# First batch of a Fourier filter and SwiGLU kernel: copies to VectorE, tables behind x in SyncE's queue, stores to ScalarE's queue

## The chip, the cores and the metric

One core of a Trainium2 chip. The time is the device time of one execution in microseconds (us), as the median of the runs of a kernel; the span of a profiled execution is about 1.8 us shorter than its time. "Faster" means by more than 2%.

## The reference, cut to what matters

```python
# x: 8 batches x 3008 x 256, filter: 1505 x 256 (real and imaginary)
X = np.fft.rfft(x, axis=1)
y = np.fft.irfft(X * (filt_r + 1j * filt_i)[None], n=3008, axis=1)
t = y.reshape(8 * 3008, 256)
g = t @ w_gate                                  # 256 -> 1536
out = (g / (1 + np.exp(-g)) * (t @ w_val)) @ w_out
```

The kernel does the Fourier transform as matmuls in three steps (3008 = 47 x 64), with a round trip through two DRAM tensors, d1 and d2, to turn the data between the steps. The dense part (gate, value, output projection) is done with a Strassen scheme of seven products. For batches 1 to 7 the spectral part is hidden in gaps of the dense part of the batch before. For batch 0 it stands alone at the front, and that front is all that this case is about.

## The kernel before

The first step, for each of 16 units: one fp32 matmul (`pa`, which the trace records as two overlapping passes, 1.06 us each in batch 0), a copy out of PSUM, a store to d1.

```python
def stage1(self, u):
    ...
    p1 = spool0 if self.b == 0 and u % 2 else t1pool
    t1 = p1.tile([NK, NV, C], FP32, ..., tag="t1", bufs=2)      # four tiles in all for batch 0
    ps = fps.tile([128, NV, C], FP32, ..., tag="f")             # two PSUM banks
    nc.tensor.matmul(out=ps[0:NK], lhsT=wf_t, rhs=self.x.pop(u), start=True, stop=True)
    nc.scalar.copy(out=t1, in_=ps[0:NK])
    queue = nc.scalar if self.b == 1 else nc.gpsimd
    queue.dma_start(out=self.d1_rows[:, ts(u, NV), :], in_=t1)
```

The tables and the filter of batch 0: three parts of one table transfer (1 MB) and four filter transfers, all 15 issued by ScalarE.

```python
def load_tables(self, parts=3):
    ...
    for i in range(parts):
        nc.scalar.dma_start(out=tb[:, ts(i, n)], in_=de_dram[:, ts(i, n)])
        for rows, view in filter_parts():                       # real: rows 0-63, imaginary: 64-127
            nc.scalar.dma_start(out=f[rows, ts(i, n), :], in_=view(n * i, n))
```

The middle step reloads d1 (`t2`), multiplies (`pb`), filters on VectorE (four operations into `p` and `q`), adds on GpSimd, multiplies back (`pc`), copies on ScalarE (`g`) and stores to d2:

```python
def stage2a(self, u):
    ...                                                         # pb into ps
    for h in (lo, hi):
        nc.vector.tensor_tensor(out=pt[h], in0=ps[h], in1=fr, op=ALU.mult)
    nc.vector.scalar_tensor_tensor(out=qt[lo], in0=ps[hi], scalar=-1.0, in1=fi, ...)
    nc.vector.tensor_tensor(out=qt[hi], in0=ps[lo], in1=fi, op=ALU.mult)
    add(nc.gpsimd, pt, pt, qt)

def stage2b(self, u):
    ...                                                         # pc into ps
    nc.scalar.copy(out=g, in_=ps)
    for p in range(2):
        queue = nc.scalar if self.b == 0 and p else nc.gpsimd   # one store each
        queue.dma_start(out=self.d2[...], in_=g[64 * p:64 * p + 64])
```

The weights come as 64-bit floats in 18 pieces and are rounded to fp32 on the chip (five VectorE operations, two on ScalarE, five on GpSimd each); two pieces are rounded before the middle step, two after the last step (`pd`), the others in the dense part.

```python
for i in range(4):
    spec.load_x(i)                     # SyncE's queue
spec.load_tables()                     # ScalarE's queue
load_weights(0); load_weights(1)       # SyncE's queue
nc.sync.dma_start(out=wi_t, in_=wi_dram.ap())
for u in range(N_ONE):
    spec.stage1(u)
for _ in range(2):
    round_weights(todo.pop(0))         # each also loads the piece after next
...                                    # middle step, stage2b three units behind stage2a
for i in range(2):
    spec.load_t4(0, i)
for step in range(4):
    spec.stage3(0, step)
for _ in range(2):
    round_weights(todo.pop(0))
```

## Time and profile before

3151.23 us, median of 4 runs (3150.08 to 3152.27); three runs had 3150.79. The front, read from the timeline (T0 is the start of the middle step's first matmul):

| milestone before | us |
|---|---|
| first matmul of the first step | 11.11 |
| first, last copy out of its PSUM banks (ScalarE) | 41.95, 68.85 |
| T0 | 77.33 |
| last filter operation on VectorE | 117.47 |
| first matmul of the last step | 133.18 |
| start of the dense part | 140.08 |
| end of the span | 3150.0 |

So there are 140 us that a better front can shorten, and 3009.9 us of dense part behind them. The prediction below shows the lines that lead to this. Two windows of 5 us while x and the tables load (columns: window, length, busy us and count of PE, PEld, DVE, ACT, POOL, then granted clock, share of the DMA engines busy, GB/s):

```profile
20.00:25.00 5.00, 0.00 (x0) 0.00 (x0) 0.00 (x0) 0.00 (x0) 0.00 (x0) 1.00 1.04 238
35.00:40.00 5.00, 0.00 (x0) 0.00 (x0) 0.76 (x2) 0.00 (x0) 0.00 (x0) 1.00 1.14 274
```

The granted clock of 1.00 in such early windows should not be read as full speed: the two passes of one `pa` take 1.99 us at 11.11 us and 1.02 us at 2542.22 us of the same trace.

### The profile page before, as it was taken

The page shows a single profiled execution, that of the slowest core. Times are in us where ns is not written, and L with a number is a line of the kernel's source. Part 1 is how long each engine was busy: PE and PEld are TensorE (multiplying, and loading weights), DVE is VectorE, ACT ScalarE, POOL GpSimd, SP SyncE. Part 2 cuts the span into 40 slices and gives each one's busy share as a digit, 9 for nine tenths or more (in the row PEclk, how much of TensorE's full clock was granted, in tenths as well). Part 3 has the DMA queues.
Part 4 walks back from the last instruction along what each step waited for, and adds up shares of the span by engine and source line. Part 5 has one row for each costly group of instructions (what it writes and reads, how often), then busy time and mean ns, then how long its engine had stood idle before and what let it go on. Part 6 is the DMA issues. An engine that isn't in the chain of part 4 may idle for free.

```text
span 3150.0 us, 41042 instructions
## 1 busy us (share of the span) xinstructions
PE 3042.9 (97%) x15488; PEld 2236.8 (71%) x15488; DVE 1461.6 (46%) x2331; ACT 1149.9 (37%) x2086; POOL 1409.8 (45%) x1634
## 2 busy tenths in 40 slices
PE   3689999999999999999999999999999999999999
PEld 1456777677777777777777677777777677777776
DVE  0665544345533445335543455434554445544443
ACT  1244333433334333433334433333333433333333
POOL 1475554345543345434444445434544345533333
PEclk9799999999999999999999999999999999999999
DMA  8432322213222223122222222221321212210000
GB/s 191 113 119 88 87 64 61 70 54 90 68 57 63 71 64 87 50 70 64 77 60 60 67 81 67 62 65 54 87 74 52 71 55 77 64 31 21 21 5 17
DMA packets 122481, 212.50 MB, mean 67 GB/s; under 512 B 23670, under 2 KB 68214, under 8 KB 121426
## 3 DMA queue, kind: packets, MB, share of 16 engines
q1 hardware_dynamic: 91388, 128.58, 14.8%
q0 software_dynamic: 25024, 70.29, 7.7%
q10 hardware_dynamic: 5872, 11.01, 1.5%
q8 instruction: 122, 2.00, 0.3%
q14 instruction: 75, 0.61, 0.1%
HBM read 134.81 MB, written 74.97 MB: 67 GB/s over the span
## 4 chain that ended last, share of the span: by engine, by line
PE 80%; POOL 8%; DVE 5%; issue 3%; DMA 2%; ACT 2%; SPq 0%; POOLq 0%; ACTq 0%; DVEq 0%
PE wA_v L419 15%; PE wA_g L419 15%; PE wA_o L483 7%; PE wE_v L419 7%; PE wE_g L419 7%; PE wE_o L483 7%; PE wF_o L483 4%; PE wF_g L419 4%; PE pd L380 4%; PE wF_v L419 3%; PE pa L319 3%; POOL o L162 3%; POOL h L165 3%; PE pc L360 3%; PE pb L340 2%
## 5 line engine op out<-in xcount | busy, mean ns | idle before, releaser
L419 PE MATMUL wA_v<-y,wv_t 128*128 128x376 f32 x1536 | 613.8, 481 | 8.6 <-ACT u_v L428 6.5
L419 PE MATMUL wA_g<-y,wg_t 128*128 128x376 f32 x1536 | 615.7, 483 | 0.9 <-ACT u_g L428 0.9
L165 POOL TENSOR_TENSOR h<-h 128x376 f32<-128x376 f32 x576 | 567.1, 985 | 28.8
L162 POOL TENSOR_TENSOR h<-h 128x376 f32<-128x376 f32 x192 | 189.0, 984 | 705.9 <-PE wE_v L419 387.7
L428 ACT COPY u_g<-wA_g 128x376 f32<-128x376 f32 x576 | 269.5, 468 | 587.3 <-PE wA_g L419 585.0
L419 PEld LDWEIGHTS wA_v<-y,wv_t 128*128 128x128 f32 x1536 | 290.7, 191 | 205.8 <-DVE h L441 15.8
L483 PEld LDWEIGHTS wA_o<-wo_t,h 128*128 128x128 f32 x3456 | 407.5, 193 | 16.5 <-issue 0.6
L483 PE MATMUL wA_o<-wo_t,h 128*128 128x128 f32 x3456 | 418.7, 276 | 0.0
L419 PEld LDWEIGHTS wA_g<-y,wg_t 128*128 128x128 f32 x1536 | 282.1, 191 | 167.2 <-issue 28.0
L446 ACT ACTIVATE s<-s 128x1128 f32<-128x1128 f32 x192 | 219.5, 1143 | 375.9 <-DVE s L162 375.9
L448 DVE TENSOR_TENSOR h<-s,h 128x1128 f32<-128x1128 f32 x192 | 256.3, 1335 | 123.4 <-ACT s L446 123.2
L419 PE MATMUL wE_v<-y,wv_t 128*128 128x376 f32 x768 | 307.9, 483 | 3.4 <-DVE h L162 3.4
L419 PE MATMUL wE_g<-y,wg_t 128*128 128x376 f32 x768 | 306.3, 481 | 1.8 <-DVE s L162 1.2
L428 ACT COPY u_v<-wA_v 128x376 f32<-128x376 f32 x576 | 272.2, 473 | 69.9 <-PE wA_v L419 66.0
L162 DVE TENSOR_TENSOR s<-u_g,wE_g 128x376 f32<-128x376 f32 x384 | 209.0, 544 | 176.8 <-ACT u_g L428 174.9
L483 PE MATMUL wE_o<-wo_t,h 128*128 128x128 f32 x2304 | 282.1, 277 | 7.5 <-DVE o L162 7.5
L162 DVE TENSOR_TENSOR s<-u_g,wF_g 128x376 f32<-128x376 f32 x192 | 104.5, 544 | 393.7 <-PE wF_g L419 375.4
L483 PE MATMUL wF_o<-wo_t,h 128*128 128x128 f32 x2304 | 278.6, 275 | 0.0
L483 PEld LDWEIGHTS wE_o<-wo_t,h 128*128 128x128 f32 x2304 | 267.7, 192 | 14.1 <-DVE o L162 13.6
L483 PEld LDWEIGHTS wF_o<-wo_t,h 128*128 128x128 f32 x2304 | 267.8, 192 | 0.3
L162 DVE TENSOR_TENSOR h<-u_v,wE_v 128x376 f32<-128x376 f32 x384 | 209.1, 545 | 28.1 <-ACT u_v L428 5.1
L419 PEld LDWEIGHTS wE_v<-y,wv_t 128*128 128x128 f32 x768 | 146.3, 191 | 102.1 <-DVE h L162 5.1
(82 smaller groups left out, 3222.7 us busy)
## 6 DMA issues: line engine op xcount, KB each, us to landing
t<-d SPq DMA_DIRECT2D x192, 128.0 KB
t<-d SPq DMA_DIRECT2D x64, 384.0 KB
d<-g POOLq DMA_DIRECT2D x180, 128.0 KB, 2.8
d<-t POOLq DMA_DIRECT2D x112, 192.0 KB, 2.4
tb<-de_tbl SPq DMA_DIRECT2D x84, 256.0 KB
x<-in_x_dram SPq DMA_DIRECT2D x112, 160.0 KB
out_dram<-o POOLq DMA_DIRECT2D x128, 128.0 KB, 2.0
f<-in_filt_r_dram SPq DMA_DIRECT2D x168, 64.0 KB
```

What stands on the lines that cost most here:

```text
L162: eng.tensor_tensor(out=dst, in0=a, in1=b, op=ALU.add)
L165: eng.tensor_tensor(out=dst, in0=a, in1=b, op=ALU.subtract)
L319: nc.tensor.matmul(out=ps[0:NK], lhsT=wf_t, rhs=self.x.pop(u), start=True, stop=True)
L340: nc.tensor.matmul(out=ps[:, i, :], lhsT=self.tb[u][:, i, 0, :], rhs=t2[:, i, :], start=True, stop=True)
L360: nc.tensor.matmul(out=ps[:, i, :], lhsT=tb[:, i, 1, :], rhs=pt[:, i, :], start=True, stop=True)
L380: nc.tensor.matmul(out=psv[:, n, :], lhsT=self.t4[k, i][:, n, ts(cb, 128)], rhs=wi_t, start=True, stop=True)
L419: nc.tensor.matmul(out=bk[z][kind], lhsT=wt[z][:, j, LEFT[p], :], rhs=y[:, RIGHT[p], :], start=start, stop=True, skip_group_check=True)
L428: nc.scalar.copy(out=u[(1, 6, 7).index(p)], in_=bk[z]["A"])
L446: nc.scalar.activation(out=s[:, 0:3], in_=s[:, 0:3], func=AF.Silu)
L448: nc.vector.tensor_tensor(out=h[:, 0:3], in0=s[:, 0:3], in1=h[:, 0:3], op=ALU.mult)
L483: nc.tensor.matmul(out=bk[kind][:, t, :], lhsT=hs[i][:, HID[p], t0:t0 + 128], rhs=wo_t[:, JB * q + i, WO[p], :], start=start and t == 0 an ...
```

## The change

The intent: nothing in the first batch's front should wait behind something else's issue. It has three parts, called A, B and C here. A: the first step's copies go to VectorE. B: the tables and the real half of the filter go behind x in SyncE's queue; ScalarE keeps the imaginary half and takes the first two weight pieces; pieces 2 and 3 load after the middle step and are kept at that place in program order (a line left out below). C: both stores of a middle unit go out on ScalarE's queue, none on GpSimd's.

```diff
 def load_tables(self, parts=3):                                           # B
-    nc.scalar.dma_start(out=tb[:, ts(i, n)], in_=de_dram[:, ts(i, n)])
+    nc.sync.dma_start(out=tb[:, ts(i, n)], in_=de_dram[:, ts(i, n)])
     for rows, view in filter_parts():
-        nc.scalar.dma_start(out=f[rows, ts(i, n), :], in_=view(n * i, n))
+        queue = nc.scalar if rows.start >= 64 else nc.sync
+        queue.dma_start(out=f[rows, ts(i, n), :], in_=view(n * i, n))
...
 def stage1(self, u):                                                      # A
-    nc.scalar.copy(out=t1, in_=ps[0:NK])
+    if self.b:
+        nc.scalar.copy(out=t1, in_=ps[0:NK])
+    else:
+        nc.vector.tensor_copy(out=t1, in_=ps[0:NK])
...
 def stage2b(self, u):                                                     # C
-        queue = nc.scalar if self.b == 0 and p else nc.gpsimd
+        queue = nc.gpsimd if self.b else nc.scalar
...
-    load_weights(0)                                                       # B
-    load_weights(1)
+    load_weights(0, nc.scalar)
+    load_weights(1, nc.scalar)
...
     for _ in range(2):
-        round_weights(todo.pop(0))
+        round_weights(todo.pop(0), False)     # do not load the piece after next here
...                                            # after the middle step
+for j in (2, 3):
+    load_weights(j)
```

More of the change, by code (lines that the diff above doesn't have):

```diff
@@ L187, with load_weights @@
     raws = {}
-    def load_weights(j):
+    def load_weights(j, queue=nc.sync):
         if j < len(weights):
@@ L192, in load_weights, with round_weights @@
             for i in range(2):
-                nc.sync.dma_start(out=raws[j][:, i], in_=weights[j][0][:, i])
-    def round_weights(j):
-        load_weights(j + 2)
+                ins = queue.dma_start(out=raws[j][:, i], in_=weights[j][0][:, i])
+                if j in (2, 3):
+                    tc.keep_in_program_order(ins)
+    def round_weights(j, following=True):
+        if following:
+            load_weights(j + 2)
         raw, (_, dst, left) = raws.pop(j), weights[j]
```

## The prediction

> **What bounds the kernel now.** I read the page first, then busy time by window, the waits of the first 200 us, and the timeline of the start.
>
> ```profile
> PE 3042.9 (97%) x15488; PEld 2236.8 (71%) x15488; DVE 1461.6 (46%) x2331; ACT 1149.9 (37%) x2086; POOL 1409.8 (45%) x1634
> PE   3689999999999999999999999999999999999999
> ```
>
> TensorE is busy 97% of the span, and the idle part sits in the first two or three of 40 slices. Busy time by window says how much is left there (columns: window, its length, busy us and count of PE, PEld, DVE, ACT, POOL; granted clock, DMA share, GB/s):
>
> ```profile
> 0.00:150.00 150.00, 76.09 (x185) 42.86 (x186) 46.54 (x74) 28.62 (x48) 42.97 (x61) 0.87 0.62 154
> ...
> 500.00:1000.00 500.00, 498.79 (x2596) 368.92 (x2596) 221.59 (x353) 188.47 (x342) 215.38 (x251) 1.00 0.23 65
> ```
>
> From 500 us on PE idles 1.2 us in 500: nothing to win there, and the change touches nothing there. What it touches is the first batch's spectral part, alone at the front: the first step's matmuls (pa) and their stores to d1, the middle step (pb, filter, pc, stores to d2), the last step (pd). The dense part starts at 140.08 us and then needs TensorE for about 3010 us. So I predict by how much that start moves.
>
> The waits (who for whom; us in total, times, longest):
>
> ```profile
> ACT L320 <- DMA raw<-in_moe_w_val_dram: 40.7, 1, 40.7
> ```
>
> The releaser named there is the last thing to land before; the real one shows in the timeline (start, duration, engine, line):
>
> ```profile
> 39.09 1.54 ACTq L303 DMA_DIRECT2D f<-in_filt_i_dram  x2
> ...
> 40.66 1.28 ACT L320 ACT_TABLE_LOAD   x1 [40.66 <-DMA raw<-in_moe_w_val_dram]
> ...
> 68.85 0.58 ACT L320 COPY t<-pa 96x512 f32<-96x512 f32 x1 [1.12 <-PE pa L319]
> ...
> 77.33 2.04 PE L340 MATMUL wA_b<-t,tb 128*128 128x256 f32 x4 [8.52 <-DMA t<-d]
> ```
>
> ScalarE issues the 15 table and filter transfers ahead of its copies, and its issue stands still whenever the queue takes no more: the last leaves at 40.6 us, and only then does ScalarE empty the first PSUM bank, though x for it landed at 11. TensorE, with two banks, sits 26 us. After that sixteen copies come at 1.71 us (two 0.86 us matmul passes each[...]), to 69.4; the middle step's first matmul starts at 77.33 (call it T0). The middle step's end:
>
> ```profile
> 106.84 0.58 ACT L364 COPY g<-pc 128x512 f32<-128x512 f32 x1 [3.40 <-PE pc L360]
> ...
> 110.52 1.27 POOL L162 TENSOR_TENSOR p<-p,q 128x512 f32<-128x512 f32 x1
> ...
> 111.85 2.08 PE L360 MATMUL pc<-p,tb 128*128 128x256 f32 x4 [2.88 <-POOL p L162]
> ...
> 113.96 0.58 ACT L364 COPY g<-pc 128x512 f32<-128x512 f32 x1 [4.38 <-PE pc L360]
> ...
> 114.84 0.60 POOL L368 DMA_DIRECT2D d<-g  x1 [3.05 <-ACT g L364]
> 115.46 1.27 POOL L162 TENSOR_TENSOR p<-p,q 128x512 f32<-128x512 f32 x1
> ...
> 133.18 7.11 PE L380 MATMUL pd<-wi_t,t 96*128 96x94 f32 x32 [7.66 <-DMA t<-d]
> ...
> 140.08 1.51 PE L419 MATMUL wA_g<-y,wg_t 128*128 128x376 f32 x2
> ```
>
> The reader is to see a loop: GpSimd's add, pc, ScalarE's copy, GpSimd's store issue, and only then the next add, though its data was ready: 115.46 - 110.52 = 4.94 us a turn. VectorE, whose four operations per turn take 2.82 us (turns begin at 86.62, 89.44, 92.27), is the limit only earlier.
>
> [...] the add at 115.46 stands 3 us behind a store of other data. [...] over the first 40 us two queues together move 210 to 225 GB/s at a DMA share of about 1. [...] Here pc of one turn takes 1.13 us at 90 us but 2.08 us at 112 us, where the loop starves it.
>
> **The change part by part.**
> *First step.* The sixteen copies leave ScalarE, whose stream blocks, for VectorE, idle until 39 us. [...] the first step runs as x arrives. x (3.08 MB) now stands first in SyncE's queue, against the imaginary filter (1.57 MB), the first two weight pieces (1.05 MB) and the d1 stores only; the 1 MB table that shared the DMA engines before is behind it. I expect x complete at 25 to 32 us and the last copy 7 us (four units of 1.71) later, 32 to 39, against 69.4.
> *What sets T0.* The reload of d1 (t2) now stands in SyncE's queue behind tables and real filter (3.15 + 1.57 MB). So T0 is set by bytes, not by the first step. Before, loads of x 3.08, table 3.15, filter 3.15, weights 1.05, small 0.07 = 10.5 MB, with six stores of 0.2 MB, were done by about 50 us (the rate then falls to the stores' own 105 to 118 GB/s): counting stores at 290 GB/s (118 GB/s at a share of 0.40 to 0.41, 60 to 70 us), 10.5 MB took 49 - 4 = 45 us, or 233 GB/s. After: 1 us to start + 45 us for the loads + 3.15 MB of stores at 290 GB/s = 10.9 us + the first 0.26 MB of t2 about 1 us + landing about 2 us: T0 = 60, against 77.33: 17.3 us saved. The first step's 30 us head start is not worth 30, as the DMA engines are full.
> *Rounding of the first two weight pieces.* About 5.3 us of VectorE operations (2 x (0.43 + 0.42 + 0.69 + 0.43 + 0.69)); it now fits between the copies' end and T0. Before, three operations lay between the filter's first and second, so filtering resumed at 81.66 rather than 80.1: 1.5 us saved.
> *Middle step.* The twelve store issues of 0.6 us leave GpSimd's stream and with them the loop. ScalarE then has 0.58 + 2 x 0.6 = 1.8 us per turn, below VectorE's 2.82, so VectorE sets the pace: T0 + 2.04 (pb) + 12 x 2.825 = 33.9 gives 95.9 for VectorE's end (before 118.15, of which 40.8 after T0; now 35.9). The last add follows at once: 1.27, so 97.2. Before it ended at 122.91, 4.8 after VectorE. Together the middle step saves 4.9 + 3.5 = 8.4 us, the 1.5 of the rounding included.
> *Tail.* From the last add to the first pd, 133.18 - 122.91 = 10.27, stays; plus an estimated 0.3 because both stores leave one after the other on ScalarE. First pd 97.2 + 10.6 = 107.8; pd to the dense start 6.9 as before: 114.7.
> *Weight pieces 2 and 3* now load after all t2 rather than between. They are needed after pd only, are on the queue from about 85 us and land by about 90: no cost.
> *The rest.* Each engine's order from pd on is unchanged, so the 3010 us shift as a block.
> **Sum:** 17.3 + 8.4 - 0.3 = 25.4 us earlier; 3150.8 - 25.4 = 3125.4 us, 0.8% less.
>
> **The rivals.**
> (a) *A queue wait takes the place of the issue wait.* If SyncE's queue, now with 8 MB of loads, gets too small a share or the mix runs at 200 GB/s, T0 moves to 68 or 70 and the gain falls to 16 us: 3135. For it: everything needed hangs on one queue in order, and 5 us windows in the first 40 us vary from 181 to 274 GB/s. Against: no other queue has work after about 40 us, so SyncE's then has the DMA engines to itself.
> (b) *The middle step stays bound by something else.* ScalarE's copies and issues, the t2 reloads (0.26 MB in and 0.26 MB out each 2.82 us, 186 GB/s) or the q buffers could hold it at 3.2 us a turn: 4.5 us lost, 3130. Against: the trace moved 215 GB/s between 85 and 90 us while VectorE kept its pace.
> (c) *More comes out.* Were the stores absorbed beside the loads for nothing, T0 would be near 50 and the time 3115. The DMA share of about 1 speaks against.
> (d) *The dense part does not move with its start*, because weight rounding, which already starves TensorE between 145 and 260 us, waits for loads. Its loads are triggered by the rounding itself, so it should move along; a disturbance of 3 to 5 us either way is possible.
>
> **Range and chances.** T0 between 54 and 68 gives -6/+8 us, the pace and (d) about 4: 3117 to 3136 holds it 8 times in 10. For 2% (63 us) the dense part would have to start at 77, which the bytes and twelve VectorE turns forbid: faster 0.01. Slower by 2% needs a stall of 60 us nobody points to: 0.01.
>
> **What would show it.** In the changed profile: VectorE copies of pa from about 6 us on, ending by 40; DMA share near 1 until 57 or so; the first pb near 60, waiting for t2; VectorE turns of 2.82 us to the end with GpSimd's adds right behind; pd near 108; the dense part from 115. A first pb past 68, or turns over 3.2 us, or a gain in the start that the end doesn't have, would prove me wrong.

## The result, and the profile after

3120.11 us, median of 4 runs (3119.17 to 3120.84), against 3151.23: 31.1 us less where 25.4 were predicted. The ratio is 0.9901, with a 95% interval of 0.9884 to 0.9918. (A ratio is the mean time of one kernel's fast runs over that of the other's of the same rounds, so not quite the ratio of the medians quoted.) The output is correct, and the mean granted clock was 0.991 in both profiles. The time lies in the predicted range of 3117 to 3136.

The page of the changed kernel, engines and then the PE row of the 40 slices:

```profile
PE 3047.5 (98%) x15488; PEld 2234.6 (72%) x15488; DVE 1473.1 (47%) x2347; ACT 1140.7 (37%) x2070; POOL 1404.6 (45%) x1622
...
PE   6799999999999999999999999999999999999999
```

VectorE has exactly 16 instructions more and ScalarE 16 fewer: the copies. GpSimd has 12 fewer: the stores. The first slice of TensorE went from 3 to 6 tenths, the second from 6 to 7.

| milestone, us | before | predicted | after |
|---|---|---|---|
| first copy of the first step | 41.95 | from about 6 | 9.25 |
| last copy of the first step (its end) | 68.85 (69.4) | (32 to 39) | 42.24 (42.9) |
| T0 | 77.33 | 60 | 52.35 |
| T0 to first matmul of the last step | 55.85 | 47.8 | 47.49 |
| first matmul of the last step | 133.18 | 107.8 | 99.84 |
| start of the dense part | 140.08 | 114.7 | 106.75 |
| dense part, to the end of the span | 3009.9 | 3010 | 3011.65 |
| span | 3150.0 | | 3118.4 |

The start, in the timeline of the changed kernel (start, duration, engine; in brackets the idle time before and what ended it):

```profile
9.25 0.69 DVE L327 COPY t<-pa 96x512 f32<-96x512 f32 x1 [8.38 <-PE pa L323]
...
42.24 0.69 DVE L327 COPY t<-pa 96x512 f32<-96x512 f32 x1 [1.28 <-PE pa L323]
...
48.80 19.49 SPq L295 DMA_DIRECT2D t<-d  x24
...
52.35 2.07 PE L347 MATMUL wA_b<-t,tb 128*128 128x256 f32 x4 [10.14 <-DMA t<-d]
```

The first copy no longer waits for ScalarE's 15 issues, the last is done 26.6 us earlier than before, and the reload of d1 is issued 6.6 us after it, once the last d1 store has landed. The same stretch by windows of the changed kernel:

```profile
20.00:25.00 5.00, 3.65 (x4) 0.79 (x4) 1.71 (x3) 0.00 (x0) 1.03 (x2) 1.00 1.02 324
25.00:30.00 5.00, 4.19 (x6) 1.03 (x5) 1.73 (x3) 0.00 (x0) 1.02 (x2) 1.00 1.06 350
...
35.00:40.00 5.00, 4.34 (x5) 0.68 (x3) 1.24 (x2) 0.00 (x0) 0.94 (x2) 1.00 1.01 367
...
45.00:50.00 5.00, 0.00 (x0) 0.00 (x0) 3.39 (x6) 1.31 (x2) 3.92 (x5) 1.00 0.53 170
```

The share is 1.02 to 1.06 where it was 1.04 to 1.14 before, yet 324 to 367 GB/s flow instead of 238 to 274. In the last line the DMA engines are already half idle, while VectorE, ScalarE and GpSimd round the first two weight pieces, nearly all of it ahead of T0. The windows from 0 to 50 us add up to 13.6 MB: all 10.5 MB of loads and the 3.15 MB of d1 stores were through by 50 us.

The end of the middle step and the start of what follows, in the timeline of the changed kernel; compare the loop of 4.94 us that the prediction shows:

```profile
85.54 1.39 DVE L355 TENSOR_TENSOR p<-wF_b,f 64x512 f32<-64x512 f32 x2
85.68 1.26 POOL L162 TENSOR_TENSOR p<-p,q 128x512 f32<-128x512 f32 x1 [1.56 <-DVE q L358]
...
88.50 1.26 POOL L162 TENSOR_TENSOR p<-p,q 128x512 f32<-128x512 f32 x1 [1.56 <-DVE q L358]
...
99.84 7.11 PE L387 MATMUL pd<-wi_t,t 96*128 96x94 f32 x32 [7.95 <-DMA t<-d]
...
106.75 1.52 PE L426 MATMUL wA_g<-y,wg_t 128*128 128x376 f32 x2
```

GpSimd's adds now follow 2.82 us apart, each released by VectorE's last operation of the turn, and no store issue lies between them.

Not all of it reaches the end: the dense part starts 33.3 us earlier, the span is 31.6 us shorter. The 1.7 us are given back between about 134 and 177 us, where the changed kernel's granted clock drops to 0.57 and 0.75 in two 5 us windows. The kernel before has such windows too (a mean of 0.66 from 180 to 190 us), so the clock is not shown to be the cause. The loss is within what the prediction's rival (d) allowed, and in a second profile of the same kernel (below) the dense part took 3009.4 us, so the runs do not establish it as a property of the change.

### The profile page after: what moved, and what is told of

Its sections match the earlier page's. It is cut to its first block, busy times and chain, and to the rows that moved or that the text cites. A ratio compares the mean times of both kernels' runs of the same rounds, so it can differ in the third digit from the quotient of the medians.

```text
span 3118.4 us, 41017 instructions
## 1 busy us (share of the span) xinstructions
PE 3047.5 (98%) x15488; PEld 2234.6 (72%) x15488; DVE 1473.1 (47%) x2347; ACT 1140.7 (37%) x2070; POOL 1404.6 (45%) x1622
## 4 chain that ended last, share of the span: by engine, by line
PE 80%; POOL 7%; DVE 6%; issue 3%; ACT 2%; DMA 2%; SPq 0%; POOLq 0%; ACTq 0%; DVEq 0%
PE wA_v L426 15%; PE wA_g L426 15%; PE wA_o L490 7%; PE wE_v L426 7%; PE wE_g L426 7%; PE wE_o L490 7%; PE wF_o L490 4%; PE wF_g L426 4%; PE pd L387 4%; PE wF_v L426 3%; PE pa L323 3%; POOL o L162 3%; POOL h L165 3%; PE pc L367 2%; PE pb L347 2%
## 5 line engine op out<-in xcount | busy, mean ns | idle before, releaser
L490 PEld LDWEIGHTS wE_o<-wo_t,h 128*128 128x128 f32 x2304 | 268.1, 192 | 14.2 <-DVE o L162 13.6
L162 POOL TENSOR_TENSOR p<-p,q 128x512 f32<-128x512 f32 x96 | 121.6, 1266 | 225.5 <-DVE q L358 225.4
```

The source lines that it names most:

```text
L162: eng.tensor_tensor(out=dst, in0=a, in1=b, op=ALU.add)
L490: nc.tensor.matmul(out=bk[kind][:, t, :], lhsT=hs[i][:, HID[p], t0:t0 + 128], rhs=wo_t[:, JB * q + i, WO[p], :], start=start and t == 0 an ...
```

## The experiments

Twelve runs were made, in three calls. The kernel before ran beside them: 3150.15, 3150.91 and 3150.73 us.

### The parts, one and two at a time

`a_copies` is the kernel before with A alone, `b_queues` B alone, `ab_no_stores` A and B, `ac_no_queues` A and C. The edits are the diff's hunks so marked, for instance for `a_copies`:

```diff
 # the kernel before
-nc.scalar.copy(out=t1, in_=ps[0:NK])
+if self.b:
+    nc.scalar.copy(out=t1, in_=ps[0:NK])
+else:
+    nc.vector.tensor_copy(out=t1, in_=ps[0:NK])
```

The others go back from the changed kernel: `ab_no_stores` takes back the one line of C, `b_queues` that and the copies, `ac_no_queues` all of B.

> Only the first part: the first step's sixteen copies on VectorE, all queues and stores as before. Theory 'issuer' (only the copies standing behind ScalarE's blocked issue mattered; loads and stores overlap): copies from about 11 us, T0 (first matmul of the middle step) at 47 to 53, limited by SyncE's load of weight piece 2, which waits for the rounding of piece 0 and so for ScalarE's issue at about 40; from T0 to the first pd about 56 as before; time about 3125 (3121 to 3129). Theory 'bytes and order' (the reordered queues were needed as well): T0 at 60 or later, time 3134 or more.

> Only the second part: tables and real filter behind x in SyncE's queue, weight pieces on ScalarE's; copies on ScalarE, stores as before. 'Issuer': ScalarE's ten issues are through by about 18 us, copies start at about 19, T0 at 50 to 55, time 3124 to 3128. 'VectorE needed' (the copies had to change engine): T0 at 60 or later, 3134 or more.

> The change with its third part undone: half of the middle step's stores back on GpSimd's queue. If the GpSimd loop costs what the prediction said, T0 stays at 52 to 53 and T0 to first pd grows from 47.5 to about 54.4, so the time is 3120.1 + 7 = 3127. Rival: the stores' move gained little because VectorE sets the pace anyway: 3121 to 3122.

> First and third part without the reordered queues. 'Issuer': T0 as in the run with the copies alone (47 to 53), T0 to first pd 47.5 to 49, time 3116 to 3122, as the whole change or better. 'Bytes and order': 3126 or more.

Measured, with the milestones of each profile:

| run | median us | ratio, 95% | less than before | T0 | T0 to last step | dense start |
|---|---|---|---|---|---|---|
| `a_copies` | 3136.80 | 0.9958 (0.9942 to 0.9975) | 13.4 | 56.06 | 62.0 | 124.99 |
| `b_queues` | 3130.91 | 0.9938 (0.9923 to 0.9953) | 19.2 | 58.49 | 52.7 | 118.08 |
| `ab_no_stores` | 3128.09 | 0.9928 (0.9914 to 0.9943) | 22.1 | 56.45 | 52.47 | 115.82 |
| `ac_no_queues` | 3128.50 | 0.9931 (0.9916 to 0.9946) | 21.7 | 56.01 | 53.85 | 116.76 |
| all (the change) | 3120.11 | 0.9901 (0.9884 to 0.9918) | 31.1 | 52.35 | 47.49 | 106.75 |

Neither theory of the expectations came out whole. `a_copies` has a T0 (56.06) between the two and the time of "bytes and order" (3136.80), `b_queues` lies between its two (58.49 and 3130.91), and `ac_no_queues` (3128.50) misses the 3116 to 3122 that unblocked copies alone should give. `ab_no_stores`, 8.0 us slower than the change, comes near the 7 that were expected, but by luck: T0 was 4 us later than expected, T0 to the last step 2 us shorter.

A alone already brings T0 to 56, although no table has moved, and B alone to 58, although the copies stay on ScalarE: so T0 before was set by the blocked copies, and neither A nor B alone is "the" cause. But A alone saves only 13.4 us in the end, because T0 to the last step grows from 55.85 to 62.0. Why, shows ScalarE's timeline in `a_copies`:

```profile
36.77 9.17 ACTq L303 DMA_DIRECT2D f<-in_filt_r_dram  x2
56.48 4.33 ACTq L303 DMA_DIRECT2D f<-in_filt_i_dram  x2
60.84 1.28 ACT L212 ACT_TABLE_LOAD   x1 [60.84 <-DMA t<-d]
```

ScalarE is still issuing transfers at 60.8 us, 20 us later than in the kernel before. Its two operations of the weight rounding stand behind those issues, and so does the rest of the rounding. `ac_no_queues` has the same stall, and its VectorE stream shows what that costs (lines 210 to 221 are the rounding, 351 to 354 the filter):

```profile
68.00 0.69 DVE L352 SCALAR_TENSOR_TENSOR q<-wA_b,f 64x512 f32<-64x512 f32 x1
68.72 0.69 DVE L221 SCALAR_TENSOR_TENSOR w<-raw,w 128x512 f32<-128x512 uint32 x1
69.33 0.42 DVE L216 TENSOR_SCALAR pw<-pw 128x512 uint32<-128x512 uint32 x1
69.78 0.68 DVE L354 TENSOR_TENSOR q<-wA_b,f 64x512 f32<-64x512 f32 x1
```

The rounding falls in the midst of the filter operations of the middle step, where VectorE is the bound (turns of 2.82 us in the change). From T0 to the last step `ac_no_queues` takes 53.85 us and the change 47.49, so 6.4 us go there; another 3.7 us lie in the later T0, but that much T0 also scatters between runs of one kernel (below). In the change ScalarE's issues are through at 17.5 us, and VectorE's part of the rounding is over at 50.5, before T0.

The stall itself is not the one that the prediction describes ("its issue stands still whenever the queue takes no more"). In `a_copies` the chain that ended last has this:

```profile
53.65 2.81 DMA t<-d
...
56.48 3.42 DMA f<-in_filt_i_dram
```

A filter transfer on ScalarE waits until a reload of d1 on SyncE has landed, which has nothing to do with it; and just before, the DMA engines were mostly idle:

```profile
50.00:55.00 5.00, 0.00 (x0) 0.00 (x0) 0.21 (x1) 0.00 (x0) 0.35 (x1) 1.00 0.29 83
```

At a share of 0.29 a full queue is hardly the reason. The list of waits of the built program (it comes from building the kernel and is no view of the profile) shows what it waits for instead. These are rows of ScalarE's and SyncE's streams of the kernel before, in program order:

```
ACT  3 L303 DMACopy f_123<-in_filt_r_dram 32x8x256
ACT  4 L303 DMACopy f_123<-in_filt_i_dram 32x2048 [waits DMAHW1_49]
ACT  5 L303 DMACopy f_123<-in_filt_i_dram 32x8x256 [waits DMAHW3_49]
SP   5 L268 DMACopy wo_t<-in_x_dram 14x1536
SP   6 L268 DMACopy wo_t<-in_x_dram 80x2048 [waits DMAHW0_49]
SP   7 L268 DMACopy wo_t<-in_x_dram 14x2048 [waits DMAHW2_49]
```

The transfers of both engines take eight semaphores, DMAHW0 to DMAHW7, in turn, and each waits until the one before it with the same semaphore has landed. The first three on ScalarE and the first five on SyncE go freely; the next ones wait: in the trace before, ScalarE's third is out by 2.12 us and its fourth leaves at 10.34. So at most eight are under way over the two queues together, and an engine that issues many transfers takes part in the waits of the other's. The same list for `a_copies` has the filter transfer that left at 56.48 wait for the semaphore that the reload of d1's second unit used last. So the list and the release by `t<-d` in the trace fit together; the number eight itself was not varied.

### Fewer issues from ScalarE, same bytes

If ScalarE's issue is what blocks, five large transfers instead of 15 free it without moving a queue or a copy.

```diff
 # the kernel before
-def load_tables(self, parts=3):
+def load_tables(self, parts=1):
```

> The kernel before with its tables and filters in one piece (5 transfers on ScalarE's queue in place of 15, same bytes, same queues). Theory 'eight tickets' (the built program lets each transfer of SyncE's and ScalarE's queues wait until the one eight earlier in their common order has landed, so the number of transfers blocks ScalarE, not their bytes): ScalarE's issues are through by about 20 us, copies start at 15 to 22, time 3124 to 3133 without any part of the change. Theory 'full queue' (the prediction's: the queue takes no more bytes): the last issue at about 40 and the time within 4 us of 3150.

3143.98 us, ratio 0.9977 (0.996 to 0.9994): 6.9 us less. Neither forecast was met: the result lies between the 3124 to 3133 of "eight tickets" and the 4 us at most of "full queue". ScalarE is free at 31.75 instead of 40.66 us and T0 comes 8.6 us earlier, at 68.74. Most of the freed time appears at T0, so the issue stall was the cause of the late first step before; but 419 GB/s flowed from 5 to 10 us (217 before), and still the first x arrived late enough for its matmul to start at 17.93 instead of 11.11. The stall is shortened and not removed; that the large transfers held x up is an inference that no run tests. In its own list the first eight transfers are six of SyncE's and two of ScalarE's, and ScalarE's third, with a wait, left only at 17.82. So the places are shown by the lists and by the release in `a_copies`; this run agrees in direction and misses the size.

### How long the loads take alone

The matrix of the first step (36 KB) is loaded last in SyncE's queue instead of first. No first step runs, so no store runs either, until all of SyncE's loads have landed. Nothing else changes.

```diff
 # the changed kernel
-nc.sync.dma_start(out=wf_t, in_=wf_dram.ap())      # ahead of x
...
 nc.sync.dma_start(out=wi_t, in_=wi_dram.ap())      # behind the tables
+nc.sync.dma_start(out=wf_t, in_=wf_dram.ap())
```

> The changed kernel, with the small matrix of the first step loaded last in SyncE's queue, so that no matmul and no d1 store runs while the 10.5 MB of loads go. Theory 'stores ride along' (loads alone run at about 233 GB/s, and in the changed kernel the d1 stores came on top at no cost): the first matmul at 44 to 49 us, windows up to there at 200 to 250 GB/s. Rival 'the new order loads faster': the first matmul at 34 to 40 us, windows at 280 GB/s or more without a store. Time not of interest (about 3148).

3149.11 us in a single look (state unknown). The first matmul of the first step, by the timeline of TensorE, and one window:

```profile
45.66 13.94 PE L323 MATMUL pa<-wo_t,wf_t 94*96 94x512 f32 x16 [45.66 <-DMA wf_t<-wf_tbl]
```

```profile
20.00:25.00 5.00, 0.00 (x0) 0.00 (x0) 0.00 (x0) 0.00 (x0) 0.00 (x0) 1.00 1.03 220
```

The nine windows to 45 us add up to 10.5 MB, in 45.66 us with the landing: 230 GB/s. That is the 45 us that the prediction gave the loads. In the changed kernel the same loads and 3.15 MB of stores were through by 50 us at the latest. From 20 to 45 us the changed kernel moved 341 GB/s on average (its five windows are 324, 350, 332, 367 and 333), this one 262 (220, 330, 264, 275, 219), at a share of about 1 in both but for this one's last window, where it is 0.87. That is a difference of 2.0 MB. The DMA view of the first 45 us tells it by queue (q1 is SyncE's, q10 ScalarE's, q0 carries the stores; then packets, MB, share of the 16 engines). The changed kernel:

```profile
q1 hardware_dynamic: 1846, 7.57, 55.2%
q10 hardware_dynamic: 2048, 2.62, 27.4%
q0 software_dynamic: 842, 2.60, 17.5%
```

`d_loads_alone`:

```profile
q1 hardware_dynamic: 2219, 7.87, 70.2%
q10 hardware_dynamic: 2048, 2.62, 28.1%
```

So 2.60 MB of stores held the loads up by 0.30 MB, an estimated 1.3 us at 230 GB/s: they went beside the loads nearly for nothing. This compares one profile with one. How far it is due to the stores' direction (to DRAM instead of from it) the runs don't tell. The share alone says little even without a store: in `d_loads_alone` 368 GB/s flowed from 40 to 42 us, mostly in packets of 8 KB, and 155 GB/s from 43 to 44, all in packets under 2 KB, at shares of 1.07 and 0.98.

### More tiles for the first step

In the changed kernel's waits (columns: us in total, times, longest) VectorE's copies stand still for stores of tiles that are to be used again, and the list of transfers says why (the last number is the median us from issue to landing of a store):

```profile
DVE t L327 <- DMA d<-t: 13.0, 8, 3.5
```

```profile
d<-t POOLq DMA_DIRECT2D x16, 192.0 KB, 7.2
```

Before, the same column had 2.3, with 7.9 for the slowest, whose landing at 50.72 released a copy: most stores before went out after 50 us, at a DMA share of 0.33 to 0.49, and now they go out among the loads, at a share of 1.01 to 1.07 from 15 to 45 us. Four tiles are too few for that. `e_t1_ten` gives ten, six of them in buffers of the middle step that are not yet in use.

```diff
 # the changed kernel
+if self.b == 0 and u % 10 >= 4:
+    tag = "p" if u % 10 < 8 else "g"
+    t1 = spool0.tile([128, NV, C], FP32, ..., tag=tag, bufs=4 if tag == "p" else 2)[0:NK]
+else:
     t1 = p1.tile([NK, NV, C], FP32, ..., tag="t1", bufs=2)
```

> The changed kernel with ten tiles for the first step's results in place of four (the six others are borrowed from tiles that the middle step uses later). If the wait for a store to free one of the four tiles (7 us from issue to landing) holds the first step, the copies end at 33 to 38 us in place of 43, T0 comes 3 to 5 us earlier, time 3115 to 3118. If the total of bytes holds T0: copies earlier, T0 and time the same within 1.5 us.

3119.14 us, ratio 0.9898 (0.9884 to 0.9913): within 1 us of the change (0.9901). It was run at another time. The waits are gone, the last copies come every 1.71 us and the last starts at 37.41, 4.8 us earlier, but T0 is 51.89 against 52.35, 14 us behind that copy. So the first step does not hold it any more. The chain shows what does:

```profile
17.82 25.10 DMA raw<-in_moe_w_val_dram
...
42.94 0.34 SPq L304
...
46.23 5.61 DMA t<-d
```

SyncE could issue the last part of the table only at 42.94, when a weight piece on ScalarE's queue had landed (one of the eight places again), and the reload stands behind that part. So two chains end nearly together: first step, last store, reload; and tables, reload. In time no gain clear of the scatter is seen. But the comparison with 52.35 may be unfair: three runs with four tiles that also issued the last table part late, at 43.77 to 44.30, had T0 at 56.44 to 57.09 (below). The ten tiles may thus be worth some 4 us of T0 in such runs; no run of the same call settles it.

### The rounding of pieces 2 and 3 ahead of the last step

VectorE is idle for 17 us between its last filter operation (88.3) and its first subtraction in the last step (105.4), and the engines that TensorE waits for early in the dense part also do the rounding (TensorE's longest waits there, between 106 and 180 us of the change, are 3.9 us for ScalarE and 3.2 for VectorE). This moves the rounding into the gap.

```diff
 # the changed kernel
 for i in range(2):
     spec.load_t4(0, i)
+for _ in range(2):
+    round_weights(todo.pop(0))
 for step in range(4):
     spec.stage3(0, step)
-for _ in range(2):
-    round_weights(todo.pop(0))
```

> Not a part of the change but a step on: the changed kernel with the rounding of weight pieces 2 and 3 placed ahead of the last step, where VectorE stands idle for 17 us. If the rounding chain is what starves TensorE after the dense part's start, the dense part gets 3 to 9 us shorter: 3111 to 3117. If the loads or the matmuls set that stretch, no change within 1.5 us.

3112.27 us, ratio 0.9875 (0.986 to 0.989), as the theory of the rounding chain had it. T0 was late here, at 57.09, and the dense part started at 111.57, later than the change's 106.75; but it took 2999.8 us instead of 3011.65. The start of the dense part is thus not the whole of the front's worth: which weights are rounded by then counts as well.

### The change and its version without C again, and a late third table part

`after_again` is the changed kernel unaltered, `ab_again` is `ab_no_stores` unaltered, on one chip. `p_third_late` issues the last third of the table and of the real filter behind the first three reload pairs, to get T0 earlier:

```diff
 # the changed kernel, load_tables: the last part's transfers in SyncE's queue are kept back
+for i in range(parts):
+    part(i, "sa" if i < parts - 1 else "a")
+self.last_part = lambda: part(parts - 1, "s")
 # stage2a
 for v in range(ahead) if u == 0 else ():
     self.load_two(v)
+if self.b == 0 and u == 0:
+    self.last_part()
```

> The changed kernel once more. The runs that share its start word for word showed T0 at 52.4 (itself), 56.5 and 57.1 us. If that is a matter of chip or call, T0 here differs from 52.4 and the time moves with it (3118 to 3125); if it belongs to the built program, T0 is 52 to 53 and the time 3119 to 3121 again.

> The change without its third part once more, beside the changed kernel on the same chip. If the stores' move is worth what the stretch from T0 to the first pd showed, it is 5 us slower than the changed kernel here; if the 8 us between the two earlier medians are right, 8 us.

> The changed kernel with the last third of table and real filter (1.57 MB) behind the first three reloads of d1 in SyncE's queue. Theory 'bytes ahead of the reload hold T0': 1.57 MB at 233 GB/s is 6.7 us less ahead of it, but the first step's last store lands at about 48 and holds T0 then: T0 2 to 5 us earlier than in the changed kernel of this call, time 2 to 5 us less. Theory 'the stores hold T0': T0 and time unchanged within 1.5 us.

| run | median us (all runs) | ratio, 95% | T0 | T0 to last step |
|---|---|---|---|---|
| `after_again` | 3122.85 (3121.91 to 3124.24) | 0.9912 (0.9895 to 0.9928) | 56.44 | 47.31 |
| `ab_again` | 3126.77 (3125.24 to 3130.04) | 0.9925 (0.9908 to 0.9942) | 53.97 | 52.49 |
| `p_third_late` | 3123.70 (3121.52 to 3124.53) | 0.9912 (0.9897 to 0.9927) | 51.09 | 52.5 |

Three things follow. First, one and the same kernel had T0 at 52.35 and at 56.44, and 3120.11 and 3122.85 us, in two calls; T0 differences of some 4 us and time differences of some 3 us between calls are no evidence. This also means that of the 7.65 us by which the prediction's T0 was late, the second profile shows only 3.6. The scatter goes with the issue of the last table part by SyncE. In the first profile of the change:

```profile
38.95 0.34 SPq L304 DMA_DIRECT2D tb<-de_tbl  x1
```

and in `after_again`:

```profile
44.30 0.34 SPq L304 DMA_DIRECT2D tb<-de_tbl  x1
```

Both wait there for a weight piece on ScalarE's queue to land, 4.7 and 6.5 us. In `after_again` the DMA share falls to 0.68 meanwhile (40 to 45 us), and the last store, behind the late table part, lands at 52.84 instead of 48.66. `ab_no_stores` and `g_round_first`, with T0 at 56.45 and 57.09, issued that part at 43.77 and 44.08; `ab_again`, with T0 at 53.97, at 36.85. Second, C is worth 5.0 us in one pair of profiles (52.47 to 47.49) and 5.2 us in the other (52.49 to 47.31), read from T0 to the last step, which T0's scatter does not touch; the medians of the same call differ by 3.9 because T0 fell the other way. Third, `p_third_late` had its T0 5.4 us earlier than `after_again` and was not faster: T0 moved as the first theory said, the time as the second. VectorE's stream shows where it went:

```profile
60.94 0.68 DVE L368 TENSOR_TENSOR q<-wF_b,f 64x512 f32<-64x512 f32 x1
66.83 1.39 DVE L365 TENSOR_TENSOR p<-wA_b,f 64x512 f32<-64x512 f32 x2 [5.21 <-PE wA_b L357]
```

After three turns VectorE stands for 5.21 us: the fourth reload stands behind the late table part. A wait ahead of T0 had become a wait after it.

### All three additions

`k_all` is the change with the ten tiles, the late third and the early rounding, each as above.

> All three steps on top of the change: ten tiles for the first step, the last third of tables late, the rounding of pieces 2 and 3 ahead of the last step. With ten tiles the first step's stores land by about 42, so if bytes and stores share in holding T0, T0 falls to 43 to 48 us, 5 to 8 us earlier; with the 8 us of the earlier rounding the time is 3103 to 3108. If T0 can't fall, 3112 as with the rounding alone.

3108.98 us (3107.92 to 3110.44), ratio 0.9866 (0.9852 to 0.9881): the fastest of all. It just misses the expectation. T0 came at 47.72, but T0 to the last step took 52.5 us with the same stop of 5.21 us after the third turn, so the late third probably gives nothing here either; the change with the tiles and the rounding alone was not run. The dense part took 2998.9 us, about 10 to 13 us less than in the two profiles of the change, so most of what it has over the change comes from the early rounding.

## Why the prediction was right or wrong

**The range: right.** The reason given, that the dense part moves with its start, held to 1.7 us. But T0 itself, 52.35 in the first profile, lies outside the 54 to 68 that the range was built on; 56.44 in the repeat lies inside.

**The first step on VectorE: right in kind, late in the end.** The copies begin at 9.25, and that the first step would not be held by a copy's length was the estimate: a copy takes 0.69 us, against 1.71 from one copy to the next where TensorE sets the pace (12.94, 14.65 and 16.36 us). The last ends at 42.9 and not between 32 and 39. The missing term is the four t1 tiles: stores took 7.2 us instead of 2.3, and copies waited 13.0 us for them. `e_t1_ten` removed the waits and the last copy started at 37.41; a gain in time was not seen beyond the scatter.

**T0: the step that failed.** The sum for T0 was 1 + 45 + 10.9 + 1 + 2 = 60 us. The small terms were estimates: the first transfers leave at 0.75 us in both traces, and from the first reload's issue to T0 it was 4.36 us before and 3.55 in the change. The 45 us for the loads was right: alone they took 45.66, at 230 GB/s against the 233 of the prediction's sum, so no change of their mean rate with the order of the queues is seen. The mis-sized term is "3.15 MB of stores at 290 GB/s = 10.9 us", added to the loads as though one byte pushed out another. In the profile of the change the last store had landed at 48.66, and 13.6 MB had moved by 50: what was left of the 10.9 us is at most 50 - 45.66 = 4.3 us, and T0 came at 52.35; by 45 us the stores had put off only 0.30 MB of loads. The DMA share near 1 that was expected until 57 ended at 45 (0.53 from 45 to 50). In the repeat the last store landed at 52.84, 7.2 us after 45.66, but with the DMA engines a third idle for 5 us in between for want of a place; T0 was 56.44, still below 60. The evidence used for the term was the DMA share of 1, and that was the mistake: the share was 1 at 220 GB/s and at 367 GB/s, and with no store at 155 and 368. Rival (c), "Were the stores absorbed beside the loads for nothing, T0 would be near 50 and the time 3115", was the closer one, and it was put aside with "The DMA share of about 1 speaks against."

**What sets T0: half right.** It was "set by bytes, not by the first step". In the change the chain runs through the first step's last store, which took 5.4 us to land among the loads; with that shortened, it ran through the table in SyncE's queue and T0 came at 51.89.

**ScalarE's stall: right that it stalls, wrong why.** By the list of waits, and by the transfer of `a_copies` that left at 56.48 after 5 us with a DMA share of 0.29, the issue stood still for want of one of eight places shared by the two queues, not because a queue was full. It was also seen as a matter of the copies alone; `a_copies` and `ac_no_queues` show that it holds up the rounding too, which then costs 6.4 us in the middle step. The prediction's term for the rounding (1.5 us) was the difference between the kernels before and after and is not touched by this, but "ScalarE is free early" is a part of B's worth that it did not count.

**The middle step and the tail: right.** 47.49 us from T0 to the last step against 47.8, with turns of 2.82 us to the end and the add right behind. `ab_no_stores` kept a turn of 4.84 us at the end and took 5.0 us longer; the prediction gave 4.9 for the loop. Rival (b) did not come about.

**The sum.** The prediction's dense start was 114.7, the measured one 106.75. Of the 7.95 us, 7.65 are T0 and 0.3 the rest. The end took back 1.7, so the span is 31.6 us shorter, and 31.1 us came out in the medians instead of 25.4.

**What stays open.** Why the weight pieces, and with them the last table part, land 5 us later in some runs of one kernel than in others; what exactly lets stores ride beside loads; whether four tiles cost time in the runs with a late table part; whether the late loads of weight pieces 2 and 3 cost nothing, as predicted, since no run moved them alone; and whether the 1.7 us in the dense part of the first profile is more than scatter.

## What to carry to other kernels

Don't add the time of stores to that of loads because the DMA engines look busy (here, at a share of about 1, 2.60 MB of stores put off 0.30 MB of loads): compare what each queue has moved by a given time with and without the stores, by taking the stores away in an experiment. When an engine that computes also issues transfers, read in the build's list of waits what each issue waits for, since here such a wait held all its later work (ScalarE's copies until 40.66 us before, its rounding until 60.84 in `a_copies`) and was for a transfer of another queue (the reload of d1 that landed at 56.46). And judge an earlier start by what is ready at that moment: an earlier T0 was lost after three turns for want of the fourth reload, while weights rounded in an idle gap made the dense part 10 to 12 us shorter with no earlier start at all.
